# Row numbers of a mixture of experts: scattered into 512-byte rows without waiting for each other, on a GpSimd whose order is written out

## The chip, the cores and the metric

The kernel runs on one core of a Trainium2 chip. The metric is the time of one launch in device microseconds, smaller being better. Five engines work side by side: TensorE (matmuls; PE in the rows), VectorE (DVE), ScalarE (ACT), GpSimd (POOL) and SyncE (SP), which only issues transfers here. GpSimd issues the transfers whose row addresses come from a table in memory (gathers and scatters); SyncE issues the rest.

## The reference

Three layers follow one another: an attention with a local window and 32 global tokens per sequence, a mixture of experts in which each token goes to one expert, and a dense layer. The kernel must give the last one's output, 2176 tokens by 512 numbers.

```python
def _attn_ref(q_l, k_l, v_l, q_g, k_g, v_g):      # 4 sequences, 8 heads, 512 local + 32 global tokens, 64 wide
    ...
    out_g = np.matmul(sm(s_g), v_all)              # global tokens see everything
    mask = np.abs(pos[:, None] - pos[None, :]) <= window   # local ones see 32 to each side, and the global
    ...
    return np.concatenate([out_g, out_l], axis=2)

def _moe_ref(x, w_gate, w1, w2):                   # 512 -> 1024 -> 512, 8 experts
    logits = x @ w_gate
    expert_idx = np.argmax(logits, axis=1)
    probs = np.exp(logits - logits.max(-1, keepdims=True))
    probs /= probs.sum(-1, keepdims=True) + 1e-09
    gate_w = probs[np.arange(N), expert_idx]
    for e in range(E):
        mask = expert_idx == e
        xe = x[mask]
        h = np.maximum(xe @ w1[e], 0.0)
        out[mask] = gate_w[mask, None] * (h @ w2[e])
    return out

def _moe2_ref(x, w_in, w_out):                     # 512 -> 2048 -> 512, every token
    h = x @ w_in
    g = np.where(h >= 1, h, np.where(h <= -1, 0.0, (h + 1) ** 2 / 4))
    return g @ w_out
```

## The kernel before, in words

**Attention** takes the first sixth of the span. It writes each token's row of 514 numbers to `xs` in device memory: 512 of the token, its gate, and its own number (which output row is its own).

**Routing.** A first group of up to 128 tokens of expert 0 (their row numbers are in `zidx`, their tile is `xz`, which is the tile `xgb2`) is worked on early, by the steps of `zsteps`, which the code takes a few at a time by `zz(n)`. For the others the kernel ranks the experts by their token counts and gives the eight ranks fixed capacities (`CAPS`, 448 down to 128 tokens). The ranks are the eight **units**, worked on in the order `ORDER`; a unit is made of one to four blocks of up to 128 tokens. An expert with more tokens than fit is finished by a slow path (`overflow`), which is skipped by a branch on `nbi`.

**A unit** goes through these steps, with the names of the rows:

- `gather`: GpSimd fetches a block's rows from `xs` into one of five tiles (`xgb0` to `xgb4`; a tile is used again by a later block).
- `weigh`: the rows are multiplied by their gates, in place (`weigh_all` does it on GpSimd; the first block of the first unit on ScalarE, which is the line with `eng is None`).
- `x_t`: TensorE turns the block (into the PSUM tile `xTp`), ScalarE and VectorE make the high and low parts of the result (`xTw` or `xTh`).
- `l1_wide` or `l1_single`: the first product, three matmuls for each of exact parts (`mm3`, PSUM tile `hp`). Beside it ScalarE and VectorE split the second weights into parts (`split_w(2, ...)`, from `w2r`), and each split lets SyncE load the next unit's.
- `l2`: the second product (PSUM tile `yp`), beside which the next unit's first weights are split (`w1r`). TensorE's order puts `x_t` of the next unit between the first and the second product. ScalarE copies the result to one of three tiles `y`, and SyncE writes that to `ys` in device memory (`y_out`).
- `put_ids`: GpSimd scatters the token numbers of a block, one number of 4 bytes for each token, to `rl`, a list in device memory in the order in which the tokens stand in `ys`. The positions are `cpos` (`zpos` for the early group). Tokens of a block stand one behind the other, so a scatter of a full block writes 512 adjoining bytes in 128 pieces.

At the end of the stage the dense layer loads token tiles back from `ys` (`load_y`, tile `yr`). `rl` is read once, as `ridf`, and gives the output rows for the last scatters (`out_dram<-acc`).

**The order.** TensorE, VectorE, ScalarE and SyncE work in the order of the code. GpSimd was left to the framework's scheduler, which by its own costs decided where each gather, weighing and scatter stands. The framework also takes two scatters to `rl` as writes of the same tensor: each waits on GpSimd until the one before it has landed, and everything behind it on GpSimd waits too.

Of the kernel before, what the change touches and what calls it, by code (L numbers as in the profile page):

```python
# [8 lines left out]
F32 = mybir.dt.float32  # L9
# [4 lines left out]
U32 = mybir.dt.uint32  # L14
AF = mybir.ActivationFunctionType
ALU = mybir.AluOpType
# [13 lines left out]
DM = H * D  # L30
S = SL + SG
N = B * S
# [5 lines left out]
BLOCKS = [(k, 128 * i, min(128, CAPS[k] - 128 * i)) for i in range(4) for k in range(8) if CAPS[k] > 128 * i]  # L38
# [9 lines left out]
XW = DM + 2  # L48
YW = DM + 1
# [74 lines left out]
def emit(tc, d, out):  # L124
    nc = tc.nc
# [3 lines left out]
    dr = top.enter_context(tc.tile_pool(name="dr", bufs=1, space=DRAM))  # L129
    xs = dr.tile([N, XW], F32, name="xs")  # L130
    ys = [dr.tile([128, NP], F32, name=f"ys{u}") for u in range(4)]
    rl = dr.tile([N, 1], F32, name="rl")


    def C(name):
# [15 lines left out]
    idx = cp.tile([128, NB], I32, name="idx")  # L151
    cpos = cp.tile([128, NB], I32, name="cpos")
# [20 lines left out]
    ap = at.enter_context(tc.tile_pool(name="ap", bufs=1))  # L173
# [304 lines left out]
    zpos = cp.tile([128, 1], I32, name="zpos")  # L478
# [49 lines left out]
    xz = xgb[2]  # L528
# [9 lines left out]
    def weigh(x, r, eng=None):  # L538
        if eng is None:
            nc.scalar.activation(x[0:r, 0:DM], x[0:r, 0:DM], AF.Copy, scale=x[0:r, DM:DM + 1])  # L540
        else:
            eng.tensor_scalar(x[0:r, 0:DM], x[0:r, 0:DM], x[0:r, DM:DM + 1], None, op0=ALU.mult)

    def put_ids(x, pos):
        r = pos.shape[0]
        nc.gpsimd.indirect_dma_start(out=rl, out_offset=bass.IndirectOffsetOnAxis(ap=pos.bitcast(U32), axis=0),
                                     in_=x[0:r], in_offset=None, bounds_check=N - 1, oob_is_err=False)

    xzT = ap.tile([128, 4, 128], F32, name="xzT")
    hz = [t[:, 0:DM].rearrange("p (f c) -> p f c", c=128) for t in (xgb[3], xz)]  # L550
# [1 line left out]
    def zsteps():  # L552
        o = ps.tile([128, 4, 128], F32, tag="to", name="ps_x", bufs=3)
        for k in range(4):
            nc.tensor.transpose(o[:, k, :], xz[:, k * 128:(k + 1) * 128], ident)
        nc.scalar.activation(xzT, o, AF.Copy)
        yield
        for g in range(2):
            o = ps.tile([128, 4, 128], F32, tag="x" if g else "s", name="zh", bufs=1 if g else 3)
            for u in range(4):  # L560
                f = slice((4 * g + u) * 128, (4 * g + u + 1) * 128)
                for k in range(4):
                    nc.tensor.matmul(o[:, u, :], lhsT=w1r[k][:, f], rhs=xzT[:, k, :], start=(k == 0), stop=(k == 3))
                    if u < 3 or k < 3:
                        yield
            nc.scalar.activation(hz[g], o, AF.Relu)
            yield
        o = ps.tile([128, 512], F32, tag="y", name="yp", bufs=2)
        for u in range(4):
            c = slice(u * 128, (u + 1) * 128)  # L570
            for f in range(8):
                nc.tensor.matmul(o[:, c], lhsT=w2r[f // 2][:, f % 2, c], rhs=hz[f // 4][:, f % 4, :], start=(f == 0), stop=(f == 7))
            if u == 2:
                yield
        yz = mp.tile([128, YW], F32, tag="y", name="y", bufs=3)
        nc.scalar.activation(yz[:, 0:DM], o, AF.Copy)
        for u in range(4):
            nc.sync.dma_start(ys[u][:, 0:128], yz[:, u * 128:(u + 1) * 128])
        put_ids(xz[:, DM + 1:XW], zpos)

    zgen = zsteps()

    def zz(n):
        for _ in range(n):
            next(zgen, None)
# [133 lines left out]
    UNITS = [[i for i, b in enumerate(BLOCKS) if b[0] == k] for k in ORDER]  # L719
# [5 lines left out]
    xg = {}  # L725

    def gather(i):
        t, r = xgb[xslot[i]], BLOCKS[i][2]
        nc.gpsimd.indirect_dma_start(out=t[0:r], out_offset=None, in_=xs,
                                     in_offset=bass.IndirectOffsetOnAxis(ap=idx[0:r, i:i + 1].bitcast(U32), axis=0))  # L730
        xg[i] = t

    zz(6)
    ranks(NE, NT, 1)
# [209 lines left out]

    def weigh_all(j):
        for i in UNITS[j]:
            weigh(xg[i], BLOCKS[i][2], nc.gpsimd)
        ids(j)

    def ids(j):  # L950
        if j < 2 and later:
            return
        for i in UNITS[j]:
            put_ids(keep.get(i, xg[i][:, DM + 1:XW]), cpos[0:BLOCKS[i][2], i:i + 1])

    later, offs, keep = [], {}, {}
    idk = mp.tile([128, 3], F32, name="idk")

    def y_out(j, y, u=None):
        k = ORDER[j]  # L960
# [9 lines left out]
    def x_t(j, a=0, b=3):  # L970
        for z in range(len(UNITS[j]))[a:b]:
            x_parts(j, z, x_turn2(j, z))
# [114 lines left out]
    def run():  # L1087
        js = list(range(len(UNITS)))

        def start():  # L1090
            positions()
            later.clear()
            for j in range(2):
                ids(j)
        later.append(start)
        for n, i in enumerate(UNITS[0]):
            r = BLOCKS[i][2]
            keep[i] = idk[:, n:n + 1]
            nc.gpsimd.tensor_copy(idk[0:r, n:n + 1], xg[i][0:r, DM + 1:XW])
        for i in UNITS[1]:  # L1100
            gather(i)
        for k in range(4):
            load_raw(1, k, 1)
        for j in js:
            nxt, nxt2 = (n if n < len(UNITS) else None for n in (j + 1, j + 2))
            single = len(UNITS[j]) == 1
            if j == 4:
                load_y(0)
                load_y(1)
            if j == 7:  # L1110
                for t in range(3, 6):
                    load_y(t)
            l1_single(j, nxt, nxt2) if single else l1_wide(j, nxt)
            if nxt is not None and not single:
                x_t(nxt)
            if nxt2 is not None:
                for i in UNITS[nxt2]:
                    gather(i)
            if j == 5:
                load_y(2)  # L1120
            if j == 2:
                while wq[0][1] is load_w:
                    f, op = wq.pop(0)
                    op(f)
            l2(j, nxt, nxt2)

    def overflow():
# [79 lines left out]
        with tc.For_i(0, NX):  # L1207
            x = xgb[2]
            nc.gpsimd.indirect_dma_start(out=x, out_offset=None, in_=xs,
                                         in_offset=bass.IndirectOffsetOnAxis(ap=ix[:, 0:1].bitcast(U32), axis=0))  # L1210
            ev = nc.sync.value_load(ex[0:1, 0:1], min_val=0, max_val=E - 1)
            at = nc.sync.value_load(sx[0:1, 0:1], min_val=0, max_val=N + 384)
            weigh(x, 128, V)
            for k in range(4):
                nc.sync.dma_start(w1r[k], raw_src(1, k, ev))
                nc.sync.dma_start(w2r[k], raw_src(2, k, ev))
            nc.scalar.activation(xf, turn(x), AF.Copy)
            for g in range(2):
                p = ps.tile([128, 4, 128], F32, tag="h", name="hp", bufs=3)
                for u in range(4):  # L1220
                    f = slice((4 * g + u) * 128, (4 * g + u + 1) * 128)
                    for k in range(4):
                        nc.tensor.matmul(p[:, u, :], lhsT=w1r[k][:, f], rhs=xf[:, k, :], start=(k == 0), stop=(k == 3))
                nc.scalar.activation(hf[:, 4 * g:4 * g + 4, :], p, AF.Relu)
            p = ps.tile([128, 512], F32, tag="y", name="yp", bufs=2)
            for u in range(4):
                c = slice(u * 128, (u + 1) * 128)
                for f in range(8):
                    nc.tensor.matmul(p[:, c], lhsT=w2r[f // 2][:, f % 2, c], rhs=hf[:, f, :], start=(f == 0), stop=(f == 7))
            y = mp.tile([128, YW], F32, tag="y", name="y", bufs=3)  # L1230
            nc.scalar.activation(y[:, 0:DM], p, AF.Copy)
            for u in range(4):
                nc.sync.dma_start(ys[u][:, bass.ds(at, 128)], y[:, u * 128:(u + 1) * 128])
            put_ids(x[:, DM + 1:XW], cx[:, 0:1])
            for z in (ex, ix, cx, sx):
                V.tensor_copy(sh, z[:, 1:NX])
                V.tensor_copy(z[:, 0:NX - 1], sh)
# [3 lines left out]
    for k in range(4):  # L1241
        split_w(1, k, None)
    zz(1)
    for i, e in zip(UNITS[0], (None, nc.gpsimd, nc.gpsimd)):
        weigh(xg[i], BLOCKS[i][2], e)
    x_t(0)
    slow = nc.values_load(nbi[0:1, 0:1], min_val=0, max_val=255)
    zz(1)
    with tc.If(slow > 0):
# [116 lines left out]
        load_y(t)  # L1366
    rid = fp.tile([128, NT], I32, name="rid")
    ridf = fp.tile([128, NT], F32, name="ridf")
    nc.sync.dma_start(ridf, rl.rearrange("(t p) o -> p (t o)", p=128))
    seq = [(ph, gi, f) for ph in range(len(phases)) for gi in range(len(groups)) for f in range(*phases[ph])]  # L1370
    lag = 3
    for s in range(len(seq) + lag):
# [71 lines left out]
```

## Time and profile before

| | us |
|---|---|
| median of 3 runs | 789.9 (788.75 to 797.05) |
| the profiled execution's own time | 792.22 |
| its span (first to last instruction) | 790.4 |
| TensorE busy in the span | 723.1 (91%) |
| GpSimd busy in the span | 149.3 (19%) |

The span has three stages: attention up to about 125 us, the mixture of experts up to about 405 us, and the dense layer to the end. TensorE is the busiest engine; its busy share says that some 67 us of the span are not covered by matmuls, and the views by stretch say where these lie. [...] Lines with an L are lines of the kernel before.

### The profile page before, as it was taken

The page shows a single profiled execution, that of the slowest core. Times are in us where ns is not written, and L with a number is a line of the kernel's source. Part 1 is how long each engine was busy: PE and PEld are TensorE (multiplying, and loading weights), DVE is VectorE, ACT ScalarE, POOL GpSimd, SP SyncE. Part 2 cuts the span into 40 slices and gives each one's busy share as a digit, 9 for nine tenths or more (in the row PEclk, how much of TensorE's full clock was granted, in tenths as well). Part 3 has the DMA queues.
Part 4 walks back from the last instruction along what each step waited for, and adds up shares of the span by engine and source line. Part 5 has one row for each costly group of instructions (what it writes and reads, how often), then busy time and mean ns, then how long its engine had stood idle before and what let it go on. Part 6 is the DMA issues. An engine that isn't in the chain of part 4 may idle for free.

```text
span 790.4 us, 16396 instructions
## 1 busy us (share of the span) xinstructions
PE 723.1 (91%) x6603; PEld 644.5 (82%) x6603; DVE 484.6 (61%) x883; ACT 335.3 (42%) x766; POOL 149.3 (19%) x186
## 2 busy tenths in 40 slices
PE   8889889899169999659999999999999999999996
PEld 4666658799159999649999889999888999998984
DVE  4677984564023457448658687875885786654443
ACT  5756663453123455346455545323332433322221
POOL 4354553811251231320000000000000000002112
PEclk9999999999679999969999999999999999999999
DMA  8777782477757999899554112110111000001111
GB/s 288 234 234 208 215 273 79 128 253 164 43 39 159 243 260 141 161 229 234 192 145 130 54 60 100 54 54 1 54 53 54 20 35 1 0 1 57 56 49 67
DMA packets 52272, 95.28 MB, mean 121 GB/s; under 512 B 10128, under 2 KB 28048, under 8 KB 50144
## 3 DMA queue, kind: packets, MB, share of 16 engines
q1 hardware_dynamic: 48704, 84.91, 40.2%
q0 software_dynamic: 3488, 9.27, 5.6%
q8 instruction: 53, 0.87, 0.5%
q14 instruction: 27, 0.22, 0.2%
HBM read 80.44 MB, written 13.72 MB: 119 GB/s over the span
## 4 chain that ended last, share of the span: by engine, by line
PE 64%; issue 14%; DMA 9%; DVE 5%; POOL 4%; ACT 2%; SPq 1%; POOLq 0%; ACTq 0%; DVEq 0%
PE fh L977 7%; PE fh L975 7%; PE fh L976 7%; PE o L976 6%; PE o L977 6%; PE o L975 6%; DMA rl<-xgb,zpos 4%; PE yp L975 4%; PE yp L976 4%; PE yp L977 3%; PE hp L977 3%; PE hp L975 3%; PE hp L976 3%; DMA ys<-y 2%; DMA ks<-in_k 2%
## 5 line engine op out<-in xcount | busy, mean ns | idle before, releaser
L1293 DVE SCALAR_TENSOR_TENSOR r<-r 128x384 f32<-128x384 f32 (+1 forms) x96 | 51.4, 535 | 113.4 <-ACT r L1292 113.4
L975 PE MATMUL o<-wh,gh 128*128 128x512 f32 x272 | 106.9, 393 | 0.8 <-ACT acc L1342 0.8
L977 PE MATMUL o<-wh,gl 128*128 128x512 f32 x272 | 107.6, 396 | 0.0
L976 PE MATMUL o<-wl,gh 128*128 128x512 f32 x272 | 107.3, 394 | 0.0
L977 PE MATMUL fh<-yh,wl 128*128 128x384 f32 (+1 forms) x320 | 104.4, 326 | 0.0
L975 PE MATMUL fh<-yh,wh 128*128 128x384 f32 (+1 forms) x320 | 104.2, 326 | 0.0
L976 PE MATMUL fh<-yl,wh 128*128 128x384 f32 (+1 forms) x320 | 104.2, 326 | 0.0
L1295 ACT ACTIVATE gh<-g 128x384 fp32r<-128x384 f32 (+1 forms) x96 | 48.8, 508 | 129.2 <-DVE g L1294 129.2
L1292 ACT ACTIVATE r<-fh,half 128x384 f32<-128x384 f32 (+1 forms) x96 | 53.9, 562 | 105.5 <-PE fh L977 104.9
L1346 POOL DMA_INDIRECT out_dram<-acc,rid x17 | 16.5, 970 | 414.6 <-DVE acc L1344 413.0
L975 PEld LDWEIGHTS fh<-yh,wh 128*128 128x128 f32 x320 | 60.2, 188 | 3.5
L976 PEld LDWEIGHTS fh<-yl,wh 128*128 128x128 f32 x320 | 60.2, 188 | 3.4
L977 PEld LDWEIGHTS o<-wh,gl 128*128 128x128 f32 x272 | 51.1, 188 | 12.4 <-DVE gl L1301 0.8
L977 PEld LDWEIGHTS fh<-yh,wl 128*128 128x128 f32 x320 | 60.2, 188 | 0.0
L975 PEld LDWEIGHTS o<-wh,gh 128*128 128x128 f32 x272 | 51.1, 188 | 9.1 <-ACT acc L1342 1.3
L976 PEld LDWEIGHTS o<-wl,gh 128*128 128x128 f32 x272 | 51.1, 188 | 8.1
L907 DVE TENSOR_TENSOR w2l<-w2r,w2h 128x1024 fp32r<-128x1024 f32 x32 | 38.9, 1222 | 24.1 <-ACT w2h L906 24.0
L1294 DVE TENSOR_TENSOR g<-r,fh 128x384 f32<-128x384 f32 (+1 forms) x96 | 51.0, 531 | 3.3
L277 ACT ACTIVATE p<-sp,mn 128x128 f32<-128x128 f32 x128 | 45.3, 374 | 18.1 <-DVE mn L262 10.9
L975 PE MATMUL yp<-hTh,w2h 128*128 128x256 f32 (+4 forms) x176 | 52.7, 299 | 0.0
L976 PE MATMUL yp<-hTl,w2h 128*128 128x256 f32 (+4 forms) x176 | 52.0, 295 | 0.0
L977 PE MATMUL yp<-hTh,w2l 128*128 128x256 f32 (+4 forms) x176 | 51.9, 295 | 0.0
(234 smaller groups left out, 1644.0 us busy)
## 6 DMA issues: line engine op xcount, KB each, us to landing
w1r<-in_w SPq DMA_DIRECT2D x32, 512.0 KB, 10.2
w2r<-in_w SPq DMA_DIRECT2D x32, 512.0 KB, 7.8
wraw<-in_wf SPq DMA_DIRECT2D x16, 1024.0 KB, 5.0
ks<-in_k SPq DMA_DIRECT2D x16, 400.0 KB, 4.8
v<-in_v SPq DMA_DIRECT2D x16, 384.0 KB, 4.6
yr<-ys SPq DMA_DIRECT2D x68, 64.0 KB, 2.1
qp<-in_q SPq DMA_DIRECT2D x16, 256.0 KB, 4.7
xs<-xr SPq DMA_DIRECT2D x8, 512.0 KB, 4.8
```

Source lines behind the costliest of these rows:

```text
L277: nc.scalar.activation(p[:, i, :], sp[:, i, :], AF.Exp, bias=mn[:, i:i + 1], scale=scale, accum_out=ss[b][:, i, h:h + 1])
L907: V.tensor_tensor(l[k], r[k], h[k].bitcast(F32), ALU.subtract)
L975: nc.tensor.matmul(o, lhsT=ah, rhs=bh, start=first, stop=False)
L976: nc.tensor.matmul(o, lhsT=ah, rhs=bl, start=False, stop=False)
L977: nc.tensor.matmul(o, lhsT=al, rhs=bh, start=False, stop=last)
L1292: nc.scalar.activation(r[:, 0:w], o[:, 0:w], AF.Relu, bias=half, scale=0.5)
L1293: nc.vector.scalar_tensor_tensor(r[:, 0:w], r[:, 0:w], 1.0, r[:, 0:w], ALU.min, ALU.mult)
L1294: nc.vector.tensor_tensor(g[:, 0:w], r[:, 0:w], o[:, 0:w], ALU.max)
L1295: nc.scalar.activation(gh[:, 0:w], g[:, 0:w], AF.Copy)
L1346: w = nc.gpsimd.indirect_dma_start(out=out, out_offset=bass.IndirectOffsetOnAxis(ap=rid[:, tt:tt + 1].bitcast(U32), axis=0), in_=a, in_off ...
```

## The change: what it does

- `rl` gets rows of 128 numbers (512 bytes) in place of one number. `put_ids` writes the last 128 columns of a block's tile, so that the token number (the tile's last column) lands in the last column of the row; the other 127 are what happens to stand in the tile, and nobody reads them. The read of `ridf` takes the last column.
- Scatters to `rl` are declared independent of each other, but for the slow path's. The gather that next uses a tile still waits for the scatter that reads it.
- GpSimd's gathers, weighings and scatters of the units are pinned in the order of the code (`pin`, the framework's `keep_in_program_order`). The early group's scatter, which stands in the last step of `zsteps`, is moved by the scheduler behind the first unit's gathers.
- The first unit's token numbers, which are put aside until `cpos` is known, go to a cleared tile of the pool `y` with 128 columns for each block (before: one column each of a small tile).
- The first unit's second block is weighed on VectorE and its third on ScalarE (before: both on GpSimd), and one more piece of the early group's work stands between the first and the second turn on TensorE.

```diff
-    rl = dr.tile([N, 1], F32, name="rl")
+    rl = dr.tile([N, 128], F32, name="rl")
...
-    def put_ids(x, pos):
+    put = []
+
+    def put_ids(x, pos, free=True):
         r = pos.shape[0]
-        nc.gpsimd.indirect_dma_start(out=rl, out_offset=bass.IndirectOffsetOnAxis(ap=pos.bitcast(U32), axis=0),
-                                     in_=x[0:r], in_offset=None, bounds_check=N - 1, oob_is_err=False)
+        w = nc.gpsimd.indirect_dma_start(out=rl, out_offset=bass.IndirectOffsetOnAxis(ap=pos.bitcast(U32), axis=0),
+                                         in_=x[0:r, x.shape[1] - 128:x.shape[1]], in_offset=None, bounds_check=N - 1, oob_is_err=False)
+        if free:
+            for z in put:
+                tc.declare_no_dep(w.ins, z.ins, reason="each row is one token's")
+            put.append(w)
+        return w
...
-            if u == 2:
-                yield
+                if (u, f) in ((2, 7), (3, 3)):
+                    yield
...
     def weigh_all(j):
         for i in UNITS[j]:
-            weigh(xg[i], BLOCKS[i][2], nc.gpsimd)
-        ids(j)
+            pin(weigh(xg[i], BLOCKS[i][2], nc.gpsimd))
+        if j > 1:
+            ids(j)
 
     def ids(j):
-        if j < 2 and later:
-            return
         for i in UNITS[j]:
-            put_ids(keep.get(i, xg[i][:, DM + 1:XW]), cpos[0:BLOCKS[i][2], i:i + 1])
+            pin(put_ids(xg[i], cpos[0:BLOCKS[i][2], i:i + 1]))
...
+    pin = tc.keep_in_program_order
...
         def start():
             positions()
-            later.clear()
-            for j in range(2):
-                ids(j)
+            for n, i in enumerate(UNITS[0]):
+                r = BLOCKS[i][2]
+                pin(put_ids(idt[:, n * 128:(n + 1) * 128], cpos[0:r, i:i + 1]))
+            ids(1)
         later.append(start)
+        idt = mp.tile([128, YW], F32, tag="y", name="y", bufs=3)
+        nc.gpsimd.memset(idt, 0.0)
         for n, i in enumerate(UNITS[0]):
             r = BLOCKS[i][2]
-            keep[i] = idk[:, n:n + 1]
-            nc.gpsimd.tensor_copy(idk[0:r, n:n + 1], xg[i][0:r, DM + 1:XW])
+            pin(nc.gpsimd.tensor_copy(idt[0:r, n * 128 + 127:n * 128 + 128], xg[i][0:r, DM + 1:XW]))
         for i in UNITS[1]:
-            gather(i)
+            pin(gather(i))
...
                 for i in UNITS[nxt2]:
-                    gather(i)
+                    pin(gather(i))
...
-    for i, e in zip(UNITS[0], (None, nc.gpsimd, nc.gpsimd)):
-        weigh(xg[i], BLOCKS[i][2], e)
-    x_t(0)
+    for n, e in enumerate((None, nc.vector, None)):
+        weigh(xg[UNITS[0][n]], BLOCKS[UNITS[0][n]][2], e)
+        x_t(0, n, n + 1)
+        if n == 0:
+            zz(1)
...
-    nc.sync.dma_start(ridf, rl.rearrange("(t p) o -> p (t o)", p=128))
+    nc.sync.dma_start(ridf, rl[:, 127:128].rearrange("(t p) o -> p (t o)", p=128))
```

GpSimd's order right behind the skipped slow path, before the change. `xgb_95`, `_96`, `_2997` and `_98` are the four tiles of unit 1, and `xgb_97` is that of unit 2's first block; `rl<-idk` are the three scatters of unit 0.

```order
L729 DMA xgb_97<-xs,idx 128x514
L542 TENSOR_SCALAR xgb_97<-xgb_97 128x512
L546 DMA rl<-idk,cpos 2176x1 x3
L546 DMA rl<-xgb_95,cpos 2176x1
L546 DMA rl<-xgb_96,cpos 2176x1
L729 DMA xgb_95<-xs,idx 128x514
L546 DMA rl<-xgb_2997,cpos 2176x1
L729 DMA xgb_96<-xs,idx 96x514
L542 TENSOR_SCALAR xgb_95<-xgb_95 128x512
L546 DMA rl<-xgb_98,cpos 2176x1
```

The same engine from unit 0's scatters on, after the change (unit 1's four gathers and weighings stand ahead of these rows in both kernels, but behind the branch now).

```order
L548 DMA rl<-y,cpos 2176x128 x3
L548 DMA rl<-xgb_95,cpos 2176x128
L548 DMA rl<-xgb_96,cpos 2176x128
L548 DMA rl<-xgb_2997,cpos 2176x128
L548 DMA rl<-xgb_98,cpos 2176x128
L737 DMA xgb_97<-xs,idx 128x514
L737 DMA xgb_95<-xs,idx 128x514
L737 DMA xgb_96<-xs,idx 96x514
L542 TENSOR_SCALAR xgb_97<-xgb_97 128x512
L548 DMA rl<-xgb_97,cpos 2176x128
```

The seven scatters of units 0 and 1 now stand together ahead of all three gathers of unit 2, where five stood ahead of the second gather and six ahead of the third.

TensorE's order around the turns of unit 0, before (`yp` here is the early group's second product).

```order
L929 MATMUL xTp<-ident,xgb_95 128x128 x4
L929 MATMUL xTp<-ident,xgb_96 128x128 x4
L929 MATMUL xTp<-ident,xgb_2997 128x64 x4
L1247 TENSOR_LOAD nbi
L572 MATMUL yp<-xgb_98,w2r_91 128x128 x2
L572 MATMUL yp<-xgb_98,w2r_92 128x128 x2
L572 MATMUL yp<-xgb_97,w2r_93 128x128 x2
L572 MATMUL yp<-xgb_97,w2r_94 128x128 x2
L1249 COMPARE_AND_BRANCH
```

And after.

```order
L936 MATMUL xTp<-ident,xgb_95 128x128 x4
L579 MATMUL yp<-xgb_98,w2r_91 128x128 x2
L579 MATMUL yp<-xgb_98,w2r_92 128x128 x2
L936 MATMUL xTp<-ident,xgb_96 128x128 x4
L936 MATMUL xTp<-ident,xgb_2997 128x64 x4
L1257 TENSOR_LOAD nbi
L579 MATMUL yp<-xgb_97,w2r_93 128x128 x2
L579 MATMUL yp<-xgb_97,w2r_94 128x128 x2
L1259 COMPARE_AND_BRANCH
```

Half of the early group's last matmuls moved from behind the third turn to between the first and the second.

## Rows read from the trace of the kernel before

**Rows 1.** Busy time by stretch: length, five engines (count), clock, DMA share, GB/s.

```profile
200.00:225.00 25.00, 1.52 (x8) 0.88 (x6) 1.91 (x3) 1.63 (x3) 8.85 (x8) 0.59 0.62 39
...
325.00:345.00 20.00, 4.71 (x23) 3.61 (x21) 4.00 (x4) 4.86 (x6) 7.19 (x6) 0.73 0.94 242
...
367.00:406.00 39.00, 39.00 (x323) 39.00 (x322) 25.91 (x32) 21.87 (x35) 0.00 (x0) 1.00 0.65 207
```

**Rows 2.** TensorE's waits, 100 to 430 us: total, times, longest.

```profile
PE xTp L929 <- POOL xgb L542: 26.8, 4, 15.3
PE xTp L929 <- ACT yr L1022: 15.5, 1, 15.5
```

**Rows 3.** GpSimd in order of time: start, us, instruction, idle before and its end.

```profile
166.11 1.06 POOL L546 DMA_INDIRECT rl<-idk,cpos  x1 [0.17 <-issue]
...
202.67 0.98 POOL L546 DMA_INDIRECT rl<-xgb,cpos  x1 [8.66 <-DMA rl<-xgb,cpos]
203.95 1.01 POOL L729 DMA_INDIRECT xgb<-xs,idx  x1 [0.30 <-issue]
211.58 1.01 POOL L546 DMA_INDIRECT rl<-xgb,cpos  x1 [6.61 <-DMA rl<-xgb,cpos]
...
214.06 1.57 POOL L542 TENSOR_SCALAR xgb<-xgb 128x512 f32<-128x512 f32 x1 [0.23 <-DMA xgb<-xs,idx]
220.77 0.97 POOL L546 DMA_INDIRECT rl<-xgb,cpos  x1 [5.15 <-DMA rl<-xgb,cpos]
...
225.35 1.03 POOL L546 DMA_INDIRECT rl<-xgb,cpos  x1 [0.18 <-issue]
```

**Rows 4.** The chain that ended last, in order of time: start, us.

```profile
226.13 0.43 PE yp L975
...
228.41 0.20 PE yp L975
...
325.41 17.80 DMA ys<-y
...
345.18 2.82 PE xTp L929 x12
348.00 0.43 PE yp L975
...
351.35 0.23 PE yp L977
```

**Rows 5.** ScalarE in order of time, at the second gap.

```profile
343.31 0.38 ACT L1070 ACTIVATE y<-yp 128x256 f32<-128x256 f32 x1 [9.47 <-DMA ys<-y]
```

**Rows 6.** SyncE in order of time.

```profile
305.83 13.54 SPq L854 DMA_DIRECT2D yr<-ys  x8
```

**Rows 7.** Transfers issued from 325 to 345 us: size each, median us to landing.

```profile
ys<-y SPq DMA_DIRECT2D x4, 128.0 KB, 17.0
```

**Rows 8.** The same, from 366 to 406 us.

```profile
w1r<-in_w SPq DMA_DIRECT2D x2, 512.0 KB, 5.5
ys<-y SPq DMA_DIRECT2D x8, 128.0 KB, 4.2
```

**Rows 9.** The same, over the whole span.

```profile
out_dram<-acc,rid POOLq DMA_INDIRECT x17, 2.7
...
rl<-xgb,cpos POOLq DMA_INDIRECT x16, 10.5
```

**Rows 10.** The same, from 142 to 152 us.

```profile
xgb<-xs,idx POOLq DMA_INDIRECT x4, 3.8
```

**Rows 11.** TensorE in order of time, at unit 0's turns.

```profile
135.45 5.63 PE L572 MATMUL yp<-xgb,w2r 128*128 128x128 f32 x48
...
143.85 0.66 PE L929 MATMUL xTp<-ident,xgb 128*128 128x128 f32 x4 [2.13 <-POOL xgb L542]
...
146.06 3.50 PE L572 MATMUL yp<-xgb,w2r 128*128 128x128 f32 x16
```

**Rows 12.** VectorE in order of time, at the same place.

```profile
142.44 0.69 DVE L934 TENSOR_TENSOR xTw<-xTp,xTw 128x512 fp32r<-128x512 f32 x1 [0.54 <-POOL idk L1099]
```

More of the change, by code (lines that the diff above doesn't have):

```diff
@@ L541, in weigh @@
         else:
-            eng.tensor_scalar(x[0:r, 0:DM], x[0:r, 0:DM], x[0:r, DM:DM + 1], None, op0=ALU.mult)
-    def put_ids(x, pos):
+            return eng.tensor_scalar(x[0:r, 0:DM], x[0:r, 0:DM], x[0:r, DM:DM + 1], None, op0=ALU.mult)
+    put = []
+    def put_ids(x, pos, free=True):
         r = pos.shape[0]
-        nc.gpsimd.indirect_dma_start(out=rl, out_offset=bass.IndirectOffsetOnAxis(ap=pos.bitcast(U32), axis=0),
-                                     in_=x[0:r], in_offset=None, bounds_check=N - 1, oob_is_err=False)
+        w = nc.gpsimd.indirect_dma_start(out=rl, out_offset=bass.IndirectOffsetOnAxis(ap=pos.bitcast(U32), axis=0),
[5 more added lines that the diff above has]
+        return w
     xzT = ap.tile([128, 4, 128], F32, name="xzT")
@@ L578, in zsteps @@
             nc.sync.dma_start(ys[u][:, 0:128], yz[:, u * 128:(u + 1) * 128])
-        put_ids(xz[:, DM + 1:XW], zpos)
+        put_ids(xz, zpos)
     zgen = zsteps()
@@ L728, in gather @@
         t, r = xgb[xslot[i]], BLOCKS[i][2]
-        nc.gpsimd.indirect_dma_start(out=t[0:r], out_offset=None, in_=xs,
-                                     in_offset=bass.IndirectOffsetOnAxis(ap=idx[0:r, i:i + 1].bitcast(U32), axis=0))
         xg[i] = t
+        return nc.gpsimd.indirect_dma_start(out=t[0:r], out_offset=None, in_=xs,
+                                            in_offset=bass.IndirectOffsetOnAxis(ap=idx[0:r, i:i + 1].bitcast(U32), axis=0))
     zz(6)
@@ L946, in weigh_all @@
         for i in UNITS[j]:
-            weigh(xg[i], BLOCKS[i][2], nc.gpsimd)
-        ids(j)
+            pin(weigh(xg[i], BLOCKS[i][2], nc.gpsimd))
+        if j > 1:
+            ids(j)
     def ids(j):
-        if j < 2 and later:
-            return
         for i in UNITS[j]:
-            put_ids(keep.get(i, xg[i][:, DM + 1:XW]), cpos[0:BLOCKS[i][2], i:i + 1])
-    later, offs, keep = [], {}, {}
-    idk = mp.tile([128, 3], F32, name="idk")
+            pin(put_ids(xg[i], cpos[0:BLOCKS[i][2], i:i + 1]))
+    later, offs = [], {}
+    pin = tc.keep_in_program_order
     def y_out(j, y, u=None):
@@ L1233, in overflow @@
                 nc.sync.dma_start(ys[u][:, bass.ds(at, 128)], y[:, u * 128:(u + 1) * 128])
-            put_ids(x[:, DM + 1:XW], cx[:, 0:1])
+            put_ids(x, cx[:, 0:1], False)
             for z in (ex, ix, cx, sx):
```

## The prediction

> **What bounds the kernel now.** I read the stretches first, to see where TensorE is idle, then its waits, then the engine that it waits for, and last the chain of waits behind the second gap.
>
> The mixture-of-experts stage has two holes [rows 1]. From 200 to 225 us TensorE is busy for 1.52 us of 25.00 and its clock falls to 0.59; all other engines are idle too, GpSimd included (8.85 us), and the transfers move only 39 GB/s. From 325 to 345 us it is busy for 4.71 us of 20.00. In the stretch from 367 to 406 us it is busy throughout, so the stage can run at TensorE's own speed. The waits name two releasers [rows 2]: 26.8 us in four waits for blocks that GpSimd weighs, and 15.5 us in one wait for a copy on ScalarE.
>
> *The first hole* is GpSimd's queue [rows 3]. A scatter of row numbers is issued in about 1 us, but the next may not start before it has landed: 8.9 us from the scatter at 202.67 to the one at 211.58, of which 6.61 is idle. The gathers of unit 2 stand between these scatters, so they go out at 203.95 and later, and TensorE starves for their blocks. How long a scatter takes follows its number of rows: the one at 220.77 has 64 rows and had landed before 225.35 (that one waited for nothing but the issue), so under 4.6 us against 8.9 for 128 rows. The pieces of one scatter go one after the other, about 70 ns each. Scatters of 2 KB rows to the output land in 2.7 us, those to `rl` in 10.5 [rows 9]. So it isn't the number of rows that is slow; it is pieces of 4 bytes side by side.
>
> *The second hole* starts with SyncE: the loads of `yr` hold its queue for 13.54 us [rows 6], because they wait for writes to `ys` that land late. The weights and the next writes go out late, one write then takes 17.80 us [rows 4], and ScalarE waits 9.47 us for the tile `y` that this write must free [rows 5]; the copy that TensorE needs stands behind it. In this stretch a 128 KB write lands in 17.0 us [rows 7]. After the last scatter to `rl` the same size lands in 4.2 us and a 512 KB load in 5.5 [rows 8]. A gather with no scatter under way lands in 3.8 us [rows 10], against 10.1 for the one issued at 203.95 and weighed at 214.06 [rows 3]. So the scatters of 4-byte pieces seem to hold up every transfer, not GpSimd alone.
>
> **The change part by part.**
>
> *Scatters no longer wait, and write 512-byte rows.* Take the worst start, 166.11 as now [rows 3]. Seven scatters then go out at 1.01 + 0.30 us each, 9.2 us, until 175.3; three gathers take 3.9 us more, the last lands after at most 10.1 us, and three weighings take 4.7: unit 2 is ready at 194, before TensorE stops at 200. So the first hole goes whole. Its price is 25.00 - 1.52 = 23.5 us, and the slow clock behind it: the six matmuls from 226.13 to 228.41 take 2.28 us where six at 0.20 would take 1.2 [rows 4], so 1.0. Sum **24.5 us**. What is late next there? The weights of units 1 and 2 were loaded before the hole, and the later ones are asked for by splits that move with TensorE, so their distance stays as it is in the stretches that run without idle time.
>
> *What a 512-byte row costs* no row shows. From below: 2.7 us for a scatter of 128 rows of 2 KB, none held up by another [rows 9]. From above: 8.9 us, if the rows still went one by one [rows 3]. I take 2.7 us, because these rows don't lie side by side any more, as the output's don't. The first hole stays closed up to (200 - 166.1 - 10.1 - 4.7)/6 = 3.2 us for 128 rows (the seven hold six full ones' rows), even if they pass in single file. [...] No row of before has 512 bytes from GpSimd.
>
> *Faster transfers for everybody.* If the scatters were what held up the writes to `ys`, these land in 4.2 us, the loads of `yr` wait for nothing, and the second hole goes: 15.5 us [rows 2], half of the turns at half clock (2.82 / 2 = 1.4), and eight matmuls from 348.00 to 351.35 at 0.42 in place of 0.23, 1.5 [rows 4]: 18.4. I leave 1.4 us for the copies on ScalarE between the product and the turns, which TensorE must await anyway: **17 us**. From below it is 0, if the traffic itself is the cause. I take the upper end: 4.2 and 5.5 us were measured in a stretch whose transfers are 0.65 busy [rows 1], and between 200 and 225 transfers were slow with almost nothing moving. [...]
>
> *Weighing of unit 0.* VectorE can begin the second block when its own part of the first is done, at 143.13, and a tensor operation of this size takes 0.69 [rows 12]; TensorE's turn starts at 143.85 now [rows 11], so the weighing itself gains nothing. The gap of 2.13 us ahead of it is filled by 8 of the 16 matmuls that take 3.50 later [rows 11], 0.22 each: **1.7 us**. Upper end: if all ran at the full clock's 5.63/48 = 0.117, 3.50 - 8 x 0.117 = 2.6. Lower end: -0.5, if the third block, now behind ScalarE's copy of the second, comes later.
>
> *Costs put at nothing.* Seven scatters ahead of unit 2's first gather: covered by the 6 us to spare above. Clearing the tile and three copies on GpSimd, some 1.5 us by its weighings of 1.57 for a tile of this size: it has idle time there. The bytes: 2208 rows by the capacities and 128 of the early group, 512 bytes each, are 1.2 MB; at the 242 GB/s of the second hole 5 us of transfers, spread over 200 us in which TensorE is the bound. `ridf` reads as many pieces of 4 bytes as before.
>
> **The sum.** 24.5 + 17 + 1.7 = 43.2. The profiled execution's own time is 792.2, so 749.0; it lies 2.3 above the median of the runs, 789.9, so the forecast is 746.7, **747 us**.
>
> **The rivals.**
>
> *The second hole stays* in whole or part, since weights, `ys`, `yr` and gathers together fill the transfer engines (0.94 busy from 325 to 345 [rows 1]). Against it: the landing times of rows 8. Whole: 789.9 - 24.5 - 1.7 = 764.
>
> *The rows still go one by one*, and without waits they pile up in the queues: this is the slower side. Six full scatters' rows at 8.9 us hold the queue for 53 us from 166.1, to 219.5; unit 2's last gather lands 10.1 later and is weighed by 234, where now the turn comes at about 225. That is 9 us more in the first hole, less 1.7, and the second stays: 797. It decides from (225 - 166.1 - 14.8)/6 = 7.4 us for 128 rows on; below that it is only less gain. For it: 512-byte rows were never timed. Against it: rows 9. [...]
>
> *The change doesn't do what it says*: the pinned order makes GpSimd wait at a gather (for a tile's scatter to land, or for TensorE's turn) with weighings behind it. Everything pinned has 6 us to spare, more in later units; if a third of the first hole came back and the second hole stayed, 764 + 8 = 772.
>
> **How the numbers follow.** All three terms come: 0.62, at 743 to 750. The second hole stays wholly or partly: 0.24, 750 to 764. New waits of GpSimd: 0.07, 765 to 782. Rows one by one: 0.07, 780 to 800. The range 742 to 765 holds the first two, 0.86. A measurement of this kernel can tell about 1%, 8 us, from no change (its three runs spread over 8.3). Faster by more than that: 0.62 + 0.24 + 0.06 = 0.92; within it 0.05; slower 0.03.
>
> **What would show it.** The stretch of the first hole must be full of matmuls at full clock, and no scatter to `rl` may wait for another. A scatter should land in 3 to 5 us. Writes to `ys` of 128 KB in units 3 to 5 should land in 4 to 7 us, and `y` should never wait for them; if these stay at 10 to 17 and the second hole with them, the third step is wrong and the traffic is the cause. At unit 0 the first product should begin about 2 us earlier. The forecast is wrong above all if 512-byte rows are slow.

## The result, and the profile after

The changed kernel takes 749.4 us (median of four runs, 748.2 to 752.9) where the kernel before took 789.9 (median of three, 788.75 to 797.05): a ratio of 0.947, 95% interval 0.939 to 0.955. A fourth run of the kernel before, 800.6 us, was a slow one and is not counted. The forecast was 747, range 742 to 765. By the medians 40.5 us are gained; the profiled execution's own time is 748.2 against 792.2, so 44.0 us less where the sum said 43.2.

Busy time by stretch, of the kernel after, in the stretches of [rows 1] (same columns), and the whole of the mixture of experts:

```profile
200.00:225.00 25.00, 25.00 (x131) 23.45 (x130) 7.62 (x10) 8.26 (x13) 11.82 (x9) 1.00 0.51 160
325.00:345.00 20.00, 20.00 (x174) 20.00 (x173) 15.07 (x16) 12.24 (x17) 0.00 (x0) 1.00 0.54 170
...
150.00:400.00 250.00, 249.62 (x1681) 239.35 (x1680) 157.69 (x198) 130.75 (x202) 65.01 (x47) 1.00 0.62 199
```

The same long stretch of the kernel before:

```profile
150.00:400.00 250.00, 210.53 (x1460) 203.41 (x1461) 124.80 (x145) 107.08 (x158) 59.97 (x48) 0.92 0.81 176
```

Both holes are gone. TensorE's idle time between 150 and 400 us falls from 39.47 to 0.38, so 39.1 of the 44.0 us are idle time of this stage; of the rest 2.5 us lie at the first unit (below), and TensorE's mean granted clock (the third figure from the end) goes from 0.92 to 1.00 of full speed. Read the last two columns too: before, the transfer engines were 0.81 busy to move 176 GB/s, after only 0.62 to move 199. The transfers got cheaper; they did not get fewer.

GpSimd in order of time, kernel after, which answers to [rows 3]:

```profile
156.22 1.61 POOL L548 DMA_INDIRECT rl<-y,cpos  x1 [0.17 <-issue]
158.14 1.17 POOL L548 DMA_INDIRECT rl<-y,cpos  x1 [0.30 <-issue]
...
165.22 0.92 POOL L548 DMA_INDIRECT rl<-xgb,cpos  x1 [0.30 <-issue]
166.45 1.60 POOL L737 DMA_INDIRECT xgb<-xs,idx  x1 [0.30 <-issue]
...
172.24 1.57 POOL L542 TENSOR_SCALAR xgb<-xgb 128x512 f32<-128x512 f32 x1 [0.68 <-DMA xgb<-xs,idx]
...
178.44 1.59 POOL L542 TENSOR_SCALAR xgb<-xgb 96x512 f32<-96x512 f32 x1
```

Seven scatters go out in 9.9 us with 0.30 us between them, and unit 2 is weighed by 180.0, long before TensorE turns its blocks at 198.48. Later, GpSimd is the one that waits for TensorE (39.2 us in three waits from 180 to 400). The rows also show that pinning doesn't write out the whole order: the code has a unit's weighings first and its scatters behind them, and here they stand in turn.

Transfers issued from 270 to 325 us, kernel after, in which the unit of [rows 7] has its turn now, and from 325 to 345:

```profile
ys<-y SPq DMA_DIRECT2D x4, 128.0 KB, 5.2
...
ys<-y SPq DMA_DIRECT2D x4, 128.0 KB, 2.4
```

The same four writes land in 5.2 us where they took 17.0.

TensorE at unit 0's turns, kernel after, which answers to [rows 11]:

```profile
136.50 5.63 PE L579 MATMUL yp<-xgb,w2r 128*128 128x128 f32 x48
...
142.41 1.06 PE L579 MATMUL yp<-xgb,w2r 128*128 128x128 f32 x8
144.47 0.63 PE L936 MATMUL xTp<-ident,xgb 128*128 128x128 f32 x4 [1.01 <-PE yp L579]
146.40 0.46 PE L936 MATMUL xTp<-ident,xgb 64*128 64x64 f32 x4 [1.29 <-ACT xgb L540]
146.94 1.13 PE L579 MATMUL yp<-xgb,w2r 128*128 128x128 f32 x8
```

From the start of the 48 matmuls to the end of the last of the 16 it is 11.57 us (148.07 - 136.50); before it was 14.11 (149.56 - 135.45, [rows 11]). So the first unit's part is worth 2.5 us here. All 16 now run at 0.13 to 0.14 us each, where they took 0.22; the granted clock from the first of the 48 to 150 us is 1.00, where it was 0.88.

### The profile page after: what moved, and what is told of

It is laid out like the page before. It is cut to its first block, busy times and chain, and to the rows that moved or that the text cites. A ratio compares the mean times of both kernels' runs of the same rounds, so it can differ in the third digit from the quotient of the medians.

```text
span 746.4 us, 16404 instructions
## 1 busy us (share of the span) xinstructions
PE 717.6 (96%) x6603; PEld 640.8 (86%) x6603; DVE 484.5 (65%) x884; ACT 335.1 (45%) x767; POOL 152.2 (20%) x185
## 4 chain that ended last, share of the span: by engine, by line
PE 66%; issue 7%; DVE 3%; POOL 1%; ACT 1%; POOLq 0%; ACTq 0%; DVEq 0%
PE fh L983 7%; PE fh L981 7%; PE fh L982 7%; PE o L983 6%; PE o L982 6%; PE o L981 6%; PE yp L981 4%; PE yp L983 4%; PE yp L982 4%; PE hp L983 4%; PE hp L981 4%; PE hp L982 4%; POOL out_dram L1356 1%; PE xTp L936 1%; DVE g L1304 1%
## 5 line engine op out<-in xcount | busy, mean ns | idle before, releaser
L983 PEld LDWEIGHTS o<-wh,gl 128*128 128x128 f32 x272 | 51.1, 188 | 12.2 <-DVE gl L1311 0.6
L914 DVE TENSOR_TENSOR w1l<-w1r,w1h 128x1024 fp32r<-128x1024 f32 x32 | 38.4, 1229 | 21.2 <-ACT w1h L913 20.7
```

The source lines that it names most:

```text
L914: V.tensor_tensor(l[k], r[k], h[k].bitcast(F32), ALU.subtract)
L983: nc.tensor.matmul(o, lhsT=al, rhs=bh, start=False, stop=last)
```

## The experiments

Ratios are to the kernel before, run beside them in the same set (its medians there 789.6, 787.5, 791.6 and 789.8 us, and 789.9 for the kernel after). "Side by side" means that a row number's 4 bytes lie directly beside its neighbour's. The last column is GpSimd's idle time from 150 to 300 us ahead of weighings, for the gathers of their blocks.

| kernel | rows in `rl` | waits | GpSimd's order | us | ratio, 95% interval | idle for gathers |
|---|---|---|---|---|---|---|
| before without waits | 4 bytes, side by side | no | scheduler | 753.4 | 0.953, 0.946 to 0.960 | 30.1 |
| before with 512-byte rows | 512 bytes | yes | scheduler | 752.4 | 0.953, 0.950 to 0.957 | 10.2 |
| after with 4-byte rows | 4 bytes, side by side | no | pinned | 760.7 | 0.964, 0.951 to 0.977 | 59.3 |
| the same, not pinned | 4 bytes, side by side | no | scheduler | 755.1 | 0.954, 0.948 to 0.960 | 33.1 |
| after with waits | 512 bytes | yes | pinned | 749.2 | 0.949, 0.941 to 0.957 | 20.0 |
| after | 512 bytes | no | pinned | 749.4 | 0.947, 0.939 to 0.955 | 14.0 |
| after, not pinned | 512 bytes | no | scheduler | 754.3 | 0.955, 0.949 to 0.960 | 8.7 |
| after, first unit as before | 512 bytes | no | pinned | 750.8 | 0.951, 0.946 to 0.957 | 14.8 |
| after, 64-byte rows | 64 bytes, side by side | no | pinned | 751.1 | 0.952, 0.947 to 0.957 | 14.1 |
| after, 512 apart | 4 bytes, 512 apart | no | pinned | 747.2 | 0.947, 0.943 to 0.950 | 13.8 |
| after, 16 apart | 4 bytes, 16 apart | no | pinned | 747.7 | 0.947, 0.942 to 0.953 | 19.0 |
| after, 8 apart | 4 bytes, 8 apart | no | pinned | 748.6 | 0.947, 0.940 to 0.954 | 27.9 |
| after, other order | 4 bytes, packed, neighbours 68 apart | no | pinned | 747.9 | 0.945, 0.938 to 0.952 | 11.8 |

In the five pinned kernels with pieces of 4 bytes GpSimd's order is not quite that of the kernel after: the scatter of unit 2's first block stands behind the first of the three gathers and ahead of the other two, and in four of them it waits for that gather (11.5 us side by side, 6.5 at 8 bytes, 4.7 at 16, 2.6 at 512; the column does not count this). These five have the same order among themselves, so what the place of the pieces does is read by comparing them with one another.

### One half of the change at a time

**The changed kernel with 4-byte rows**, which still don't wait:

```diff
-    rl = dr.tile([N, 128], F32, name="rl")
+    rl = dr.tile([N, 1], F32, name="rl")
...
-                                         in_=x[0:r, x.shape[1] - 128:x.shape[1]], in_offset=None, ...
+                                         in_=x[0:r, x.shape[1] - 1:x.shape[1]], in_offset=None, ...
...
```

> The changed kernel, but each row number is written as one piece of 4 bytes side by side with the others, as before; the scatters still do not wait for each other and GpSimd's order stays pinned. Theory (pieces of 4 bytes side by side go one after the other, about 70 ns each, and hold up every other transfer): the seven scatters of units 0 and 1 pile up for some 50 us, unit 2's gathers land behind them, the first gap is back with 15 us or more, writes to ys land in 10 us or more and the second gap is back: 780 to 800 us. Rival A (only the waiting of GpSimd cost time): as the changed kernel, 748 to 753 us, no gap. Rival B (side-by-side pieces are slow for their own scatter, but hold nobody else up): the first gap is back, the second is not: 765 to 780 us.

Measured: 760.7 us from two runs (756.5 and 765.0; the rows below are of the slower). This lies between the ranges of rival A and rival B, so none of the three came as stated. GpSimd in order of time, of this kernel:

```profile
155.89 1.79 POOL L548 DMA_INDIRECT rl<-y,cpos  x1 [0.53 <-DVE cpos L931]
...
165.06 0.93 POOL L548 DMA_INDIRECT rl<-xgb,cpos  x1 [0.30 <-issue]
166.30 1.01 POOL L737 DMA_INDIRECT xgb<-xs,idx  x1 [0.30 <-remote]
178.76 1.01 POOL L548 DMA_INDIRECT rl<-xgb,cpos  x1 [11.45 <-DMA xgb<-xs,idx]
```

The gather issued behind the seven scatters has landed by 178.5 (178.76 less the 0.30 of an issue), 22.6 us after the first scatter went out. Had the rows gone one after the other at 8.9 us for 128, it would have been more than 53. So scatters of this kind do overlap when they are allowed to, but each transfer near them stays slow: the gather took about 12 us, as did the four scatters of unit 1 ahead of it (median 12.4). Stretch, TensorE and ScalarE of this kernel:

```profile
250.00:300.00 50.00, 42.59 (x327) 42.21 (x326) 24.14 (x27) 20.51 (x31) 17.28 (x12) 0.90 0.85 175
```

```profile
263.24 0.53 PE L981 MATMUL hp<-xTh,w1h 128*128 128x192 f32 x1 [3.55 <-DVE hTl L1003]
```

```profile
261.75 0.46 ACT L1076 ACTIVATE y<-yp 128x352 f32<-128x352 f32 x1 [13.36 <-DMA ys<-y]
...
291.68 0.33 ACT L1076 ACTIVATE y<-yp 128x192 f32<-128x192 f32 x1 [13.03 <-DMA ys<-y]
```

The first hole is closed, and a small relative of the second is here: ScalarE waits 13 us twice for a late write to `ys`, the halves of `h` behind it come late, and TensorE idles 7.4 us at a clock that falls to 0.90.

**The changed kernel with waits** (the lines that free a scatter of earlier ones are left out):

```diff
-        if free:
-            for z in put:
-                tc.declare_no_dep(w.ins, z.ins, reason="each row is one token's")
-            put.append(w)
```

> The changed kernel, but the scatters to rl wait for each other again, in the pinned order. Theory (with rows of 512 bytes a scatter lands in 5 us and holds nobody up): the chain of seven takes about 35 us from 156 us on, unit 2's last block is ready at about 205 us where its turn comes at 198, so a gap of 5 to 10 us remains, the second gap does not come back: 753 to 765 us. Rival A (the waiting was the cost): first gap back at 20 us or more, 770 us or more. Rival B (waiting does not matter at all once rows are 512 bytes): 748 to 753 us.

Measured: 749.2 (two runs, 746.6 and 751.8), the same as with no waits. GpSimd in order of time, of this kernel:

```profile
158.37 1.77 POOL L548 DMA_INDIRECT rl<-y,cpos  x1 [0.53 <-DVE cpos L927]
165.48 0.99 POOL L548 DMA_INDIRECT rl<-y,cpos  x1 [5.34 <-DMA rl<-y,cpos]
...
188.46 1.70 POOL L548 DMA_INDIRECT rl<-xgb,cpos  x1 [2.03 <-DMA rl<-xgb,cpos]
190.46 1.01 POOL L733 DMA_INDIRECT xgb<-xs,idx  x1 [0.30 <-issue]
...
199.52 3.12 POOL L542 TENSOR_SCALAR xgb<-xgb 128x512 f32<-128x512 f32 x2
```

The chain of seven takes 30 us from its first issue to its last, where it took 54.7 before (220.77 - 166.11, [rows 3]), and TensorE waits only 0.6 us for a block: unit 2 is weighed at 202.6, just in time. The hole that I expected did not come. With rows whose median landing is 3.0 to 4.9 us (scatters issued from 150 to 340 us) the waits alone cost nothing that these runs can tell.

**The kernel before with 512-byte rows only** (scatters wait, the scheduler's order, first unit as before; `idt` and the row size of the changed kernel):

> The kernel before with rows of 512 bytes alone: scatters wait for each other, GpSimd's order is the scheduler's, the first unit's gates are on GpSimd. Theory (the row size is most of the gain): second gap gone (17 us), first gap shrunk from 24 us to 5 to 12 us, the 2 us at unit 0 not gained: 757 to 770 us. Rival A (waiting or the order is most of it): 775 us or more. Rival B (the row size is all of it): 750 to 754 us.

Measured: 752.4, which is the range of rival B. TensorE's waits from 100 to 430 us, of this kernel:

```profile
PE xTp L929 <- POOL xgb L542: 4.7, 4, 2.0
```

It waited 26.8 [rows 2]. GpSimd's order from unit 0's scatters on is that of the kernel before, so the row size alone brings 37 us (789.6 - 752.4).

**The kernel before without waits only** (4-byte rows side by side, the scheduler's order, first unit as before; the edit is the one above, the other way round):

> The kernel before with one thing changed: scatters of row numbers no longer wait for each other; 4 bytes side by side, the scheduler's order, the first unit as before. If waiting made most of the first hole: 758 to 770, no wait of TensorE over 5 us for a block that GpSimd weighs, landings still 8 to 12 us. If the waits alone are worth little, since every landing stays slow: 775 to 790, with a hole of 10 us or more left.

Measured: 753.4, so without the waits 38 us are gained (791.6 - 753.4), more than either expectation. It is not one thing alone: once the waits are gone the scheduler orders GpSimd differently, and eight scatters go out in a row from 168.67 to 179.69, ahead of three gathers. TensorE's waits from 150 to 420 us, of this kernel:

```profile
PE xTp L935 <- POOL xgb L542: 3.6, 2, 2.6
PE xTp L935 <- ACT yr L1028: 1.0, 1, 1.0
```

Transfers issued from 265 to 290 us (size, median us to landing), and then from 300 to 420, of this kernel:

```profile
ys<-y SPq DMA_DIRECT2D x4, 96.0 KB, 8.8
...
xgb<-xs,idx POOLq DMA_INDIRECT x2, 8.5
rl<-xgb,cpos POOLq DMA_INDIRECT x2, 9.1
```

```profile
ys<-y SPq DMA_DIRECT2D x11, 128.0 KB, 2.6
```

While scatters run, landings stay slow, 8.5 to 9.1 us here, and ScalarE still waits for writes to `ys`, 9.2, 8.5 and 6.3 us at a time up to 282 us. One of these waits:

```profile
260.68 0.46 ACT L1076 ACTIVATE y<-yp 128x352 f32<-128x352 f32 x1 [8.53 <-DMA ys<-y]
```

TensorE does not run dry for it (it is busy for all of 250 to 300 us), so a late write to `ys` is not by itself a hole. But the last scatter goes out at 281.9, where the kernel before had one at 352.8. After 300 a 128 KB write lands in 2.6 us. So the second hole (325 to 345) was there because the waits had pushed the slow scatters into that stretch. Either half of the change removes both holes, and the halves don't add: by the medians 37 and 38 us alone, 40.5 together, and the whole change also has the 2.5 us of the first unit in it. What the second half adds is not clear of the noise (ratios 0.953 and 0.953 against 0.947, with intervals that overlap).

### What makes such a row slow

**Each 4-byte piece in 512 bytes of its own** (the positions are multiplied by 128, and nothing is written in between; the early group's positions, the bounds and the read follow, not shown):

```diff
-    rl = dr.tile([N, 128], F32, name="rl")
+    rl = dr.tile([N * 128, 1], F32, name="rl")
...
-        V.tensor_tensor(cpos, a, b, ALU.add)
+        V.tensor_tensor(a, a, b, ALU.add)
+        V.tensor_single_scalar(cpos, a, 128.0, op=ALU.mult)
...
```

> The changed kernel, but each row number is one piece of 4 bytes in a row of 512 bytes of its own (positions times 128). It tells what is slow, the piece's size or that neighbours share a line. Theory (sharing is what puts them one after the other): as the changed kernel, 748 to 755 us, a scatter lands in 3 to 7 us, no gap. [...]

Measured: 747.2, against 760.7 side by side in the same order of GpSimd. Pieces of 4 bytes in places of their own do as well here as rows of 512 (749.4); their size is not what cost. Busy time from 150 to 300 us, side by side and then 512 apart:

```profile
150.00:300.00 150.00, 142.59 (x919) 138.52 (x919) 72.56 (x91) 64.23 (x99) 63.48 (x47) 0.96 0.87 183
...
150.00:300.00 150.00, 150.00 (x1014) 145.59 (x1013) 84.65 (x102) 74.98 (x111) 62.54 (x46) 1.00 0.67 222
```

**Rows of 64 bytes, side by side** (`rl` is [N, 16]):

> The changed kernel with rows of 64 bytes in place of 512, still side by side, nothing waits. If what was slow is several pieces in one stretch of 64 bytes or less: as the changed kernel, 747 to 751, a scatter of 128 rows lands in 3 to 6 us and there is no hole. If the rows have to be 512 bytes apart (or of 512 bytes): as the 4-byte rows without waits, 755 to 762, a scatter lands in about 10 us and y waits for ys.

Measured: 751.1, within the spread of the changed kernel; GpSimd waits 14.1 us for gathers, as with 512 bytes (14.0). 64 bytes between two row numbers are enough here.

**4-byte pieces, 16 bytes apart** (factor 4 in place of 128):

> The changed kernel with pieces of 4 bytes, 16 bytes apart, four of them in each 64 bytes; nothing waits. If the cost is of pieces that lie directly side by side: 746 to 750, as with each piece in 512 bytes of its own. If it is of pieces that share 64 bytes: between, 750 to 757, a scatter lands in 5 to 9 us. If 512 bytes must lie between: 757 to 765, 10 us or more.

Measured: 747.7. GpSimd waits 19.0 us for gathers, a little more.

**4-byte pieces, 8 bytes apart** (factor 2):

> The changed kernel with pieces of 4 bytes, 8 bytes apart; nothing waits. Pieces 16 bytes apart cost nothing, pieces 4 bytes apart some 11 us. If only pieces that directly follow each other in memory are slow: 745 to 750. If it is pieces that share 16 bytes: 750 to 758, and a scatter of 128 rows lands in 6 to 9 us.

Measured: 748.6 in time, but in between in landings. Scatters issued from 155 to 166 us and the waits of GpSimd from 150 to 300 us, of this kernel:

```profile
rl<-xgb,cpos POOLq DMA_INDIRECT x4, 7.4
```

```profile
POOL xgb L542 <- DMA xgb<-xs,idx: 27.9, 6, 7.2
```

That slack is hidden from TensorE, which is busy for all of 150 to 300 us, so the total can't show it. The distance works by degrees in these kernels: ahead of weighings GpSimd waits 59.3, 27.9, 19.0 and 13.8 us for gathers at 4, 8, 16 and 512 bytes.

**Packed as before, in another order** (row r of `rl` goes to place (r mod 128) x 17 + r div 128, and is read back so, which is not shown):

```diff
-        V.tensor_tensor(cpos, a, b, ALU.add)
+        V.tensor_copy(cpos, a)
+        V.tensor_single_scalar(cti, cpos, 7, op=ALU.logical_shift_right)
+        V.tensor_single_scalar(cpos, cpos, 127, op=ALU.bitwise_and)
+        V.scalar_tensor_tensor(a, cpos, float(NT), cti, ALU.mult, ALU.add)
+        V.tensor_tensor(cpos, a, b, ALU.add)
...
```

> The changed kernel with the row numbers packed as tightly as before (4 bytes each, nothing between them), but stored in another order, so that neighbouring pieces of one scatter go to places 68 bytes apart. Nothing waits. If it is neighbours in one scatter, under way at the same time, that hold each other up: 745 to 750, gathers and writes to ys land as in the changed kernel. If a tight array is slow however it is written: 757 to 765, as with the 4-byte rows side by side without waits.

Measured: 747.9. Scatters issued from 155 to 166 us, of this kernel, and of the kernel after in the same stretch:

```profile
rl<-xgb,cpos POOLq DMA_INDIRECT x4, 4.0
```

```profile
rl<-xgb,cpos POOLq DMA_INDIRECT x4, 5.4
```

The array is as tight as before, 4 bytes a row, and its scatters land in 4.0 us, where they took 12.4 in the order side by side. GpSimd's order is that of the other pinned kernels with 4-byte pieces. So it is neighbours of one scatter that hold each other up when they go to adjoining places, and the gathers near them too: GpSimd's idle time ahead of weighings is 11.8 us here, and 59.3 side by side.

### The two small parts

**First unit as before**: its second and third block weighed on GpSimd (pinned), all turns first.

```diff
-                if (u, f) in ((2, 7), (3, 3)):
+                if (u, f) == (2, 7):
...
-    for n, e in enumerate((None, nc.vector, None)):
-        weigh(xg[UNITS[0][n]], BLOCKS[UNITS[0][n]][2], e)
-        x_t(0, n, n + 1)
-        if n == 0:
-            zz(1)
+    for n, e in enumerate((None, nc.gpsimd, nc.gpsimd)):
+        w0 = weigh(xg[UNITS[0][n]], BLOCKS[UNITS[0][n]][2], e)
+        if e is not None:
+            tc.keep_in_program_order(w0)
+    x_t(0)
```

> The changed kernel with only the first unit's part undone: its second and third block are weighed on GpSimd again, in pinned order, and all turns come ahead of the remaining 16 matmuls of the early group. By the prediction's last term 1.7 us slower (bounds 0.5 faster to 2.6 slower): 749 to 752, the first product about 1.7 us later after the attention's end. If the matmuls only change places: the same time within 0.5 us. This is below what three rounds can tell; the profile's start of the first product decides.

Measured: 750.8, which the interval doesn't tell from the changed kernel. TensorE in order of time, of this kernel:

```profile
135.47 5.63 PE L579 MATMUL yp<-xgb,w2r 128*128 128x128 f32 x48
...
143.59 1.10 PE L936 MATMUL xTp<-ident,xgb 128*128 128x128 f32 x4 [2.05 <-POOL xgb L542]
...
145.75 3.78 PE L579 MATMUL yp<-xgb,w2r 128*128 128x128 f32 x16
```

The wait of 2.05 us and the 16 matmuls at 0.24 us are back: 14.06 us from the first to the last row (149.53 - 135.47) against 11.57. That is the 2.5 us again.

**No pinned order**:

```diff
-    pin = tc.keep_in_program_order
+    pin = lambda w: w
```

> The changed kernel with GpSimd's order left to the scheduler instead of pinned; row size, waits and first unit as changed. If the pinned order carries part of the gain (gathers of unit 2 would go out late or behind a wait): 752 to 770, with a wait of TensorE for blocks that GpSimd weighs of more than 3 us. If the row spacing does all: 747 to 752, no wait over 3 us.

Measured: 754.3 (751.4 to 756.4), in the set in which pieces 16 apart gave 747.7 (746.0 to 750.1) with the order pinned. Busy time in one stretch of this kernel:

```profile
150.00:200.00 50.00, 46.55 (x274) 44.53 (x274) 24.99 (x36) 21.19 (x34) 35.57 (x32) 0.94 0.66 214
```

No block comes late from GpSimd, but TensorE is idle 3.45 us here and its clock is 0.94, against 0.10 us and 1.00 in the kernel after. Of the idle time 0.5 us ends with a half of `h` from VectorE; for 2.7 us the profile names no releaser. So what the order does there was not settled. The profiled run is the slowest of the four, and the intervals of the two kernels just overlap (0.949 to 0.960 and 0.942 to 0.953), so the size is uncertain too.

**4-byte rows side by side, no waits, no pinned order**, to see why the pinned one (760.7) was slower than the kernel before without waits (753.4):

> The changed kernel with 4-byte rows side by side, no waits, and GpSimd's order left to the scheduler; so the kernel before with no waits, plus the first unit's part. The kernel before without waits gave 753.4, the pinned one of the same rows 760.7. If the pinned order bunches the scatters and so holds up the writes to ys until TensorE runs dry: 749 to 755, and ScalarE waits at most 10 us for a write to ys. If the order is not it: 758 to 764, with waits of 13 us as there.

Measured: 755.1, with one wait of 10.8 us for a write to `ys` and TensorE busy throughout from 250 to 300, where the pinned version lost 7.4 us. So the order may cost something while transfers are slow, but this is not shown: the intervals overlap (0.948 to 0.960 and 0.951 to 0.977), and the pinned version's two runs lie 8.5 us apart. Nor do the pins bunch the scatters more at the start: without them eight go out by 175 us, six of these from 166 on, with them seven from 155.89 to 165.06.

## Why the prediction was right

**The total and its terms.** Between the two profiled executions 44.0 us came where 43.2 were summed; by the medians it is 40.5, and the forecast of 747 was 2.4 short of 749.4. Runs of the kernel before lie 8.3 us apart, so that the sum is met to 0.8 us is luck, and that the holes go whole is not. The two holes, 24.5 + 17 us, are 39.1 us of idle time and some 3 of slow clock (44.0 less 39.1 and 2.5, plus about 1.0 because the work ahead of the first unit took longer in this run: the 48 matmuls start at 136.50 against 135.45, [rows 11]). The first unit was put at 1.7 us and measured 2.5, near its upper bound of 2.6; the mis-sized piece is the 8 matmuls left behind the turns, taken at 0.22 us each and now at 0.14, with the granted clock at 1.00 where it was 0.88.

**The step "what a 512-byte row costs"** held within its bounds: 2.7 us was taken, bounds 2.7 to 8.9, and a scatter lands in 4.1 us from 175 to 190, with 5.4 to 6.5 in the bunch of seven. So the 2.7 was too low, and 3.2, up to which the hole should stay closed in single file, was passed as well; neither cost time here. The reason given was right and is now shown: not the number of rows, but pieces of 4 bytes side by side. The place where the prediction stopped short is "side by side" itself: 8 bytes of distance (748.6 us), or another order (747.9), would have done, and 512 bytes are not needed. Nor did the size of a piece cost anything that shows here: pieces of 4 bytes, 512 apart, took 747.2 us in all and rows of 512 bytes took 749.4.

**The step "scatters no longer wait"** was priced together with the row size. It is enough for the first hole, but not needed: 38 us come with the waits gone and the rows as before (GpSimd's order changed with them), 37 with the rows changed and the waits kept. The start of 166.11 that it took was not met either: the scatters begin at 156.22, and unit 2 is weighed by 180.0 and not 194, 14 us of room that the sum did not need. This step's fall-back, that the hole stays closed up to 3.2 us for 128 rows in single file, was too strict: with waits the chain ran at 5.0 us each ((188.46 - 158.37) / 6), and the hole stayed closed, because the chain began at 158.4 and not 166.1, and the three gathers behind it were weighed 12.2 us after the first went out (202.64 - 190.46), not 3.9 + 10.1 + 4.7.

**The step "faster transfers for everybody"** named the right rows and the right size, but it is only one of two ways. The kernel before without waits has landings of 8.5 to 9.1 us and no second hole, because its last scatter goes out at 281.9. That slow scatters do delay the writes to `ys` is shown by the 4-byte rows in pinned order, where ScalarE waited 13 us twice and TensorE ran dry; with the pieces 512 apart, in the same order, it never waited for one, nor did it in the kernel after. With the pieces side by side a gather took about 12 us beside scatters of 12.4; in what way slow pieces hold up the transfers beside them, no run here shows.

**The rivals.** "The second hole stays" did not come, and its price of 764 counted the two holes as independent; in the kernel before without waits both went, with landings that were still 8.5 to 9.1 us. "The rows still go one by one" was wrong in its price: without waits, seven side-by-side scatters and a gather were through in 22.6 us, not 53 and more, and even that form of row gave 760.7 and not 797. The 70 ns for each piece that the prediction read from [rows 3] was the pace of a single scatter in flight, not of the queues. "New waits of GpSimd" did not come; it waits for TensorE.

## What to carry to other kernels

When a scatter writes small neighbouring pieces, look at what lands beside it: here the sign was a high busy share of the transfer engines at few bytes (0.87 at 183 GB/s, against 0.67 at 222), and spreading the places (747.2 us) or reordering them (747.9) did as well as making the pieces larger (749.4). Two holes in one engine may be one delay, seen twice (here either half of the change alone gave 37 or 38 us, both 40.5); remove each suspected cause alone before adding their prices, and look whether the removal also moved the order. A pace read from operations that wait for one another need not hold when they go side by side: 8.9 us for one scatter of 128 rows in single file would have made 53 for six, and seven with a gather were through in 22.6.

## What was not expected of the hardware

Adjoining 4-byte writes of one scatter slowed the transfers near them: from 150 to 300 us, in kernels that differ only in the places of the pieces, the transfer engines are 0.87 busy at 183 GB/s with 4-byte pieces side by side, 0.74 at 220 with 8 bytes of distance, 0.69 at 221 with 16 and 0.67 at 222 with 512. In an equally tight array whose neighbours come from different scatters it is 0.67 at 222. Which unit does the holding up can't be told from these runs.
